# First pair's loads over two hardware queues, with a decay matrix as its mask: one change to a fused attention and feed-forward kernel

## The chip, the cores and the metric

One core of one Trainium2 chip. The metric is device time in microseconds (us), from the median of several executions. All numbers are of runs in the fast state unless a text says otherwise. "The span" is the time from the first to the last instruction in the profiled execution; it lies some 1.8 us under the time.

## The reference

Retention attention (a recurrence with one decay per head), then a feed-forward block with the activation h cos(h):

```python
B, H, S, D = 4, 8, 768, 64
gamma = 1.0 - 2.0 ** (-5.0 - arange(H));  scale = 1 / sqrt(D)
for t in range(S):
    state = gamma * state + outer(k[:, :, t], v[:, :, t])
    y[:, :, t] = scale * (q[:, :, t] @ state)
x = y.transpose(0, 2, 1, 3).reshape(3072, 512)
h = x @ w_in                      # 512 x 2048
out = (h * cos(h)) @ w_out        # 2048 x 512
```

The inputs q, k, v and the weights are fp32 in device memory; the kernel computes in bf16.

## The kernel before

The recurrence is done in chunks of 128 tokens. A *pair* is one chunk of two batches; there are 12 pairs. For each pair, q is scaled by gamma^t (`conv_q`), v by gamma^-t (`conv_v`), k only cast (`conv_k`); TensorE transposes q and k (`stage_t`), forms the scores (`stage_a`), VectorE multiplies them by a 0/1 mask (`stage_m`), TensorE makes the outputs and the running state (`stage_y`). `attend` is scores and mask products of both batches. `pair_f` and `unit_f` are the feed-forward's first product, `unit_o` its second. `warm(n)` issues n filler matmuls that are meant to keep TensorE's clock up (e6 below: 1.00 from 9 to 12 us with nine more of them, 0.50 in e5 without). Each load of q, k or v is 262 KB, in rows of 64 fp32 (256 bytes). In this text q0 is q of batch 0 of the first pair, and q0' is q of batch 0 of the second.

```python
def load(eng, p, names):                       # one DMA for each name
    ...
        eng.dma_start(out=t[SLOT[p]][b],
                      in_=src[2 * bp + b, :, ds(c * C, C)].rearrange("h t d -> t h d"))

load(nc.sync, 0, ("q0", "k0", "q1"))           # five loads on SyncE's queue
load(nc.sync, 1, ("q0", "v0"))
load(nc.gpsimd, 0, ("k1",))                    # the others on GpSimd's
...
load(nc.gpsimd, 0, ("v0", "v1"))
...
load(nc.gpsimd, 1, ("k0", "q1", "k1", "v1"))
for r in range(4):
    load_w_in(r)                               # 512 KB each after the cast
conv_v(1, nc.gpsimd)
for r in range(3):
    load_w_out(r)
...
warm(10)
conv_q(0, nc.vector)
conv_k(0, True)                                # True: on ScalarE
conv_v(0, nc.vector)
stage_t(0, False)                              # both copies on ScalarE
warm(3)
attend(0)
conv_k(1, True)
conv_q(1, nc.vector)
warm(6)
stage_y(0, nc.scalar.copy)
warm(2)
stage_t(1, None)                               # both copies on VectorE
attend(1)
pair_f(0, 0, (0,))                             # feed-forward, waits for w_in
stage_y(1, nc.scalar.copy)
pair_f(0, 0, (1,))
pair_f(1, 0)                                   # from here solid TensorE work
```

Of the kernel before, what the change touches and what calls it, by code (L numbers as in the profile page):

```python
# [10 lines left out]
FP32 = mybir.dt.float32  # L11
BF16 = mybir.dt.bfloat16
AF = mybir.ActivationFunctionType
ALU = mybir.AluOpType
# [16 lines left out]
def kernel(  # L31
# [9 lines left out]
    nc = tc.nc  # L41
    B, H, S, D = q.shape
    C = 128
    NC = S // C
# [19 lines left out]
    def sb(shape, dt, name):  # L64
        return const.tile(shape, dt, name=name)
# [6 lines left out]
    pos = sb([128, NC], FP32, "pos")  # L72
    halfpi = sb([128, 1], FP32, "halfpi")
    lnsc = sb([128, 1], FP32, "lnsc")
    sb([128, 1], FP32, "pad")

    w_in_sb = [sb([128, KIN, 512], BF16, f"w_in{r}") for r in range(4)]
    w_out_sb = sb([128, KOUT, DM], BF16, "w_out_sb")
# [19 lines left out]
    lgp = sb([128, NC, H], FP32, "lgp")  # L98
    gq = sb([128, NC, H], FP32, "gq")
    gk = sb([128, NC, H], FP32, "gk")  # L100


    SRC = {"q": (qf, q), "k": (kf, k), "v": (vf, v)}
# [3 lines left out]
    def load(eng, p, names):  # L107
        bp, c = divmod(p, NC)
        for n in names:
            t, src = SRC[n[0]]  # L110
            b = int(n[1])
            eng.dma_start(  # L112
                out=t[SLOT[p]][b],
                in_=src[2 * bp + b, :, ds(c * C, C)].rearrange("h t d -> t h d"))

    def load_w_in(r):
        nc.gpsimd.dma_start(
            out=w_in_sb[r],
            in_=moe_w_in[:, ts(r, 512)].rearrange("(i p) f -> p i f", p=128))
# [6 lines left out]
    def w_in_t(i, f):  # L126
        return w_in_sb[f // 4][:, i].rearrange("p (m j) -> p j m", j=4)[:, f % 4, :]


    load(nc.sync, 0, ("q0", "k0", "q1"))  # L130
    load(nc.sync, 1, ("q0", "v0"))
    load(nc.gpsimd, 0, ("k1",))
    nc.gpsimd.iota(pos, pattern=[[C, NC]], base=1, channel_multiplier=1,
                   allow_small_or_imprecise_dtypes=True)
    load(nc.gpsimd, 0, ("v0", "v1"))
    make_identity(nc, ident)
    nc.vector.memset(zero, 0.0)  # L137
    nc.vector.memset(lnsc, math.log(scale))
    nc.vector.memset(halfpi, math.pi / 2.0)
    nc.vector.memset(mask, 1.0)  # L140
    for h in range(H):
        nc.vector.tensor_scalar(out=lgp[:, :, h], in0=pos, scalar1=float(lg[h]),
                                scalar2=None, op0=ALU.mult)
    nc.scalar.activation(out=gq, in_=lgp, func=AF.Exp, bias=lnsc)
    nc.scalar.activation(out=gk, in_=lgp, func=AF.Exp, scale=-1.0)
    nc.scalar.activation(out=cosb[0][:, :8], in_=lgp[:, 0, :], func=AF.Sin, scale=0.0)
    for t in stb:
        nc.vector.memset(t, 0.0)
    nc.gpsimd.affine_select(out=mask, in_=mask, compare_op=ALU.is_ge, fill=0.0,
                            base=0, pattern=[[1, 128]], channel_multiplier=-1)  # L150


    def bc(g, c):
# [2 lines left out]
    def conv_q(p, eng):  # L156
        for b in range(2):
            eng.tensor_tensor(out=qs[p % NB][:, b], in0=qf[SLOT[p]][b],  # L158
                              in1=bc(gq, p % NC), op=ALU.mult)

    def conv_v(p, eng):
        for b in range(2):
            eng.tensor_tensor(out=vs[p % NB][:, b], in0=vf[SLOT[p]][b],  # L163
                              in1=bc(gk, p % NC), op=ALU.mult)
# [5 lines left out]
            else:  # L170
                nc.vector.tensor_copy(out=ks[p % NB][:, b], in_=kf[SLOT[p]][b])

    def stage_t(p, split, fill=0):
        n = p % NB
        for b in range(2):
            if fill:
                warm(fill * b)
            bank = banks.take()
            tr = bank.bitcast(BF16).rearrange("p (w a t) -> p w a t", w=2, a=HP)
            for w, src in enumerate((qs[n], ks[n])):  # L180
                for a in range(HP):
                    nc.tensor.transpose(tr[:, w, a, :], src[:, b, 2 * a : 2 * a + 2, :], ident)  # L182
            if split is None or split and b == 1:
                nc.vector.tensor_copy(out=qkt[n][:, :, b], in_=tr)  # L184
            else:
                nc.scalar.copy(out=qkt[n][:, :, b], in_=tr)
            banks.give(bank)

    def stage_t_dma(p):
        n = p % NB  # L190
# [11 lines left out]
    def stage_a(p, b):  # L202
# [8 lines left out]
                                 tile_position=(po, 0))  # L211
        return b, bk, ap

    def stage_m(p, item):
        b, bk, ap = item
        for j in range(2):
            nc.vector.tensor_tensor(  # L217
                out=am[p % 2][b][j], in0=ap[j],
                in1=mask.unsqueeze(1).to_broadcast([128, HP, 128]), op=ALU.mult)
            banks.give(bk[j])  # L220

    def stage_y(p, copy_st=nc.vector.tensor_copy):
        c = p % NC
        n = p % NB
        for b in range(2):
            bank = banks.take()
            yp = bank.rearrange("p (a t) -> p a t", a=HP)
            for a in range(HP):
                if c > 0:
                    for j in range(2):  # L230
                        nc.tensor.matmul(  # L231
                            yp[ts(j, 64), a, :], lhsT=stb[p % 2][:, b, a, ts(j, 64)],
                            rhs=qt(n, b, a), start=True, stop=False,
                            skip_group_check=True)
                for j in range(2):
                    nc.tensor.matmul(  # L236
                        yp[ts(j, 64), a, :], lhsT=vs[n][:, b, 2 * a + j, :],
                        rhs=am[p % 2][b][j][:, a, :], start=(c == 0), stop=True,
                        skip_group_check=True)
            nc.scalar.copy(out=xt[(p // 2) % 2][:, :, ts(2 * (p % 2) + b, C)], in_=yp)  # L240
            banks.give(bank)
        if c == NC - 1:
            return
        for b in range(2):
            for a in range(HP):
                for j in range(2):
                    h = 2 * a + j
                    nc.tensor.matmul(  # L248
                        st_ps[ts(j, 64), b, a, :], lhsT=ks[n][:, b, h, :],
                        rhs=vs[n][:, b, h, :], start=(c == 0 and b == 0 and a == 0),  # L250
                        stop=True, skip_group_check=True)
        for j in range(2):
            copy_st(out=stb[(p + 1) % 2][ts(j, 64), :, :, ts(j, 64)], in_=st_ps[ts(j, 64)])  # L253
# [62 lines left out]
    def warm(n):  # L316
        for _ in range(n):
            nc.tensor.matmul(spare, lhsT=zero[:, :128], rhs=zero, start=True, stop=True,  # L318
                             skip_group_check=True)
# [2 lines left out]
        for it in [stage_a(p, b) for b in range(2)]:  # L322
            stage_m(p, it)

    load(nc.gpsimd, 1, ("k0", "q1", "k1", "v1"))
    for r in range(4):
        load_w_in(r)
    conv_v(1, nc.gpsimd)
    for r in range(3):
        load_w_out(r)  # L330
    load(nc.gpsimd, 2, ("k0", "q0", "k1", "q1"))
# [2 lines left out]
    load(nc.gpsimd, 3, ("k0", "q0", "k1", "q1", "v0", "v1"))  # L334

    warm(10)
    conv_q(0, nc.vector)
    conv_k(0, True)
    conv_v(0, nc.vector)
    stage_t(0, False)  # L340
    warm(3)
    attend(0)
    conv_k(1, True)
    conv_q(1, nc.vector)
    warm(6)
    stage_y(0, nc.scalar.copy)
    warm(2)
    stage_t(1, None)
    attend(1)
    banks.give(spare)  # L350
    pair_f(0, 0, (0,))
# [8 lines left out]
    for part in range(3):  # L360
        for j in range(4):
            unit_o(0, j, part)
            if part == 2 and j == 0:
                stage_t(2, None)
                conv_v(2, nc.vector)
            elif part == 2 and j == 1:
                stage_m(2, stage_a(2, 0))
            elif part == 2 and j == 3:
                stage_m(2, stage_a(2, 1))
# [9 lines left out]
        if j == 1:  # L379
            stage_y(2, nc.scalar.copy)  # L380
    pair_f(2, 0)
    stage_t(3, None)
    pair_f(2, 1)
    attend(3)
    conv_q(4, nc.gpsimd)
# [97 lines left out]
```

## Time and profile before

| | before |
|---|---|
| time, median of 3 | 212.1 us (211.08 to 212.9) |
| span of the profiled execution | 210.7 us |
| TensorE busy | 200.9 us (95%) |
| mean granted TensorE clock | 0.99 |
| solid TensorE work begins | 20.02 us |
| TensorE's longest wait in the first 26 us | 1.5 us |

TensorE is busy 95% of the span, and without a gap worth naming from 20 us on. So the table's fifth row is the one to watch: what the first 20 us give or take should move the whole end by nearly as much. The views that show it stand in the prediction below.

### The profile page before, as it was taken

To read this page: it belongs to the slowest core of one execution; us is meant where nothing else is said; L and a number is where in the kernel's file an instruction comes from. 1 tells how busy PE (TensorE), PEld (TensorE's weight loads), DVE (VectorE), ACT (ScalarE), POOL (GpSimd) and SP (SyncE) were. 2 spreads that over 40 slices of the span, in tenths; PEclk is the share of its full clock that TensorE was granted. 3 is DMA by queue.
4 is the path that set the end of the run, shared out by engine and by line. 5 is a ranking of instruction groups with operands and counts; after the bars stand their busy time and mean duration, and the time that the engine had idled before them with its cause. 6 is when DMAs were issued, how large, how long until landed. Compare 5 with 4: busy or idle time off the path is not lost.

```text
span 210.7 us, 4125 instructions
## 1 busy us (share of the span) xinstructions
PE 200.9 (95%) x1614; PEld 113.0 (54%) x1637; DVE 115.0 (55%) x187; ACT 113.6 (54%) x183; POOL 84.3 (40%) x98
## 2 busy tenths in 40 slices
PE   7698999999999999999999999999999999999992
PEld 2357654548998554555455455445455444444440
DVE  5397686171976755859585484484482333343000
ACT  5664885219799336656745745745545554553110
POOL 7996238499968907999251500000000000000000
PEclk9889999999999999999999999999999999999999
DMA  6999999999999999999978321331101101110121
GB/s 163 325 246 206 215 260 287 341 255 334 272 190 212 213 305 243 238 284 181 321 165 200 92 63 50 87 67 50 50 3 50 50 3 50 50 50 27 74 92 60
DMA packets 55845, 33.83 MB, mean 161 GB/s; under 512 B 47249, under 2 KB 49553, under 8 KB 55825
## 3 DMA queue, kind: packets, MB, share of 16 engines
q1 hardware_dynamic: 49472, 17.70, 36.0%
q0 software_dynamic: 6208, 15.73, 29.1%
q8 instruction: 13, 0.21, 0.4%
q10 hardware_dynamic: 144, 0.13, 0.2%
q14 instruction: 8, 0.06, 0.1%
HBM read 27.26 MB, written 6.29 MB: 159 GB/s over the span
## 4 chain that ended last, share of the span: by engine, by line
PE 90%; DVE 4%; DMA 3%; issue 1%; SPq 0%; ACT 0%; DVEq 0%
PE bank L296 40%; PE bank L270 31%; PE bank L282 8%; PE bank L209 3%; DMA qf<-in_q_dram 3%; PE bank L231 2%; PE bank L236 2%; DVE am L217 2%; PE bank L182 1%; DVE qs L158 1%; PE st_ps L248 1%; PE bank L318 1%; SPq L112 0%; DVE qkt L184 0%; DVE ob L303 0%
## 5 line engine op out<-in xcount | busy, mean ns | idle before, releaser
L265 DVE TENSOR_TENSOR gt<-bank,cosb 128x512 bf16<-128x512 f32 x96 | 65.6, 690 | 63.5 <-ACT cosb L261 63.1
L261 ACT ACTIVATE cosb<-bank,halfpi 128x512 bf16<-128x512 f32 x96 | 65.4, 687 | 53.2 <-PE bank L270 41.4
L296 PE MATMUL bank<-w_out_sb,gt 128*128 128x512 bf16 x372 | 91.8, 379 | 1.1 <-issue 0.5
L270 PE MATMUL bank<-xt,w_in 128*128 128x512 bf16 x294 | 73.7, 380 | 0.4
L296 PEld LDWEIGHTS <-gt 128*128 128x128 bf16 x384 | 36.7, 98 | 42.7
L270 PEld LDWEIGHTS <-w_in 128*128 128x128 bf16 x304 | 33.8, 114 | 30.8 <-issue 0.2
L217 DVE TENSOR_TENSOR am<-bank,mask 128x512 bf16<-128x512 f32 x48 | 30.3, 682 | 1.0 <-PE bank L209 0.8
L158 POOL TENSOR_TENSOR qs<-qf,gq 128x512 bf16<-128x512 f32 x18 | 18.5, 1046 | 22.2 <-DMA qf<-in_q_dram 14.9
L308 ACT COPY ob<-bank 128x512 f32<-128x512 f32 x23 | 13.4, 586 | 23.3 <-PE bank L296 23.2
L112 POOL DMA_DIRECT2D kf<-in_k_dram x23 | 20.8, 906 | 3.2 <-DMA w_out_sb<-in_moe_w_out_dram 2.1
L163 POOL TENSOR_TENSOR vs<-vf,gk 128x512 bf16<-128x512 f32 x20 | 21.0, 1067 | 0.9 <-DMA vf<-in_v_dram 0.8
L282 PE MATMUL bank<-xt,w_in 128*128 128x256 bf16 x160 | 18.6, 273 | 0.0
L169 ACT CAST ks<-kf 128x512 bf16<-128x512 f32 x24 | 13.8, 615 | 7.3 <-DMA kf<-in_k_dram 7.3
L282 PEld LDWEIGHTS <-w_in 128*128 128x128 bf16 x160 | 17.1, 114 | 0.5
L112 POOL DMA_DIRECT2D vf<-in_v_dram x16 | 14.2, 887 | 4.3 <-DMA w_out_sb<-in_moe_w_out_dram 4.3
L240 ACT CAST xt<-bank 128x512 bf16<-128x512 f32 x24 | 13.0, 587 | 3.6 <-DVE gt L265 3.0
L236 PE MATMUL bank<-am,vs 128*64 128x128 bf16 x192 | 11.8, 220 | 0.3 <-DVE am L217 0.3
L231 PEld LDWEIGHTS <-stb 128*64 128x64 bf16 x160 | 8.7, 109 | 4.3 <-issue 3.8
L231 PE MATMUL bank<-qkt,stb 128*64 128x128 bf16 x160 | 10.6, 222 | 0.0
L236 PEld LDWEIGHTS <-vs 128*64 128x64 bf16 x192 | 10.0, 110 | 0.9 <-DVE am L217 0.4
L253 DVE CAST stb<-st_ps 64x512 bf16<-64x512 f32 x12 | 8.2, 687 | 3.5 <-PE st_ps L248 3.3
L318 PE MATMUL bank<-gt 128*128 128x512 bf16 x20 | 8.3, 565 | 1.3 <-DVE gt L137 1.3
(38 smaller groups left out, 70.6 us busy)
## 6 DMA issues: line engine op xcount, KB each, us to landing
kf<-in_k_dram POOLq DMA_DIRECT2D x23, 256.0 KB, 5.5
out_dram<-ob SPq DMA_DIRECT2D x23, 256.0 KB, 2.2
qf<-in_q_dram SPq DMA_DIRECT2D x19, 256.0 KB, 6.3
vf<-in_v_dram POOLq DMA_DIRECT2D x16, 256.0 KB, 6.2
vf<-in_v_dram SPq DMA_DIRECT2D x8, 256.0 KB, 5.7
w_in<-in_moe_w_in_dram POOLq DMA_DIRECT2D x4, 512.0 KB, 9.8
w_out_sb<-in_moe_w_out_dram POOLq DMA_DIRECT2D x4, 512.0 KB, 13.2
qf<-in_q_dram POOLq DMA_DIRECT2D x5, 256.0 KB, 6.8
```

The source lines that it names most:

```text
L112: eng.dma_start(out=t[SLOT[p]][b], in_=src[2 * bp + b, :, ds(c * C, C)].rearrange("h t d -> t h d"))
L158: eng.tensor_tensor(out=qs[p % NB][:, b], in0=qf[SLOT[p]][b], in1=bc(gq, p % NC), op=ALU.mult)
L163: eng.tensor_tensor(out=vs[p % NB][:, b], in0=vf[SLOT[p]][b], in1=bc(gk, p % NC), op=ALU.mult)
L169: nc.scalar.copy(out=ks[p % NB][:, b], in_=kf[SLOT[p]][b])
L217: nc.vector.tensor_tensor(out=am[p % 2][b][j], in0=ap[j], in1=mask.unsqueeze(1).to_broadcast([128, HP, 128]), op=ALU.mult)
L231: nc.tensor.matmul(yp[ts(j, 64), a, :], lhsT=stb[p % 2][:, b, a, ts(j, 64)], rhs=qt(n, b, a), start=True, stop=False, skip_group_check=True)
L236: nc.tensor.matmul(yp[ts(j, 64), a, :], lhsT=vs[n][:, b, 2 * a + j, :], rhs=am[p % 2][b][j][:, a, :], start=(c == 0), stop=True, skip_grou ...
L261: nc.scalar.activation(out=cb, in_=bank, func=AF.Sin, bias=halfpi)
L265: nc.vector.tensor_tensor(out=out, in0=bank, in1=cb, op=ALU.mult)
L270: nc.tensor.matmul(bank, lhsT=w_in_t(i, f), rhs=xt[g % 2][:, i, :], start=(i == 0), stop=(i == KIN - 1))
L282: nc.tensor.matmul(bank[:, ts(e, 256)], lhsT=w_in_t(i, f + e), rhs=xt[g % 2][:, i, ts(hf, 256)], start=(i == 0 and e == 0), stop=(i == KIN ...
L296: nc.tensor.matmul(bank, lhsT=gt[g % 2][:, f, ts(j, 128)], rhs=w_out_sb[:, f, :], start=(f == 0), stop=(f == KOUT - 1))
```

## The change

The intent is to start the solid stretch earlier. The first pair's q and k are loaded over two hardware queues, SyncE's and ScalarE's, two each. They are cast plainly; the scaling by gamma is put into a decay matrix by which the scores are multiplied in place of the 0/1 mask, so that no cast waits for the decay vectors. VectorE copies transposed banks as 32-bit words. GpSimd makes the decayed v of the first pair (needed for the state only; the outputs use the plain cast `vu`). The diff, cut to its core:

```diff
-    load(nc.sync, 0, ("q0", "k0", "q1"))
-    load(nc.sync, 1, ("q0", "v0"))
-    load(nc.gpsimd, 0, ("k1",))
+    load(nc.sync, 0, ("q0", "k0"))
+    load(nc.scalar, 0, ("q1", "k1"))
+    load(nc.sync, 1, ("k0", "q0"))
+    load(nc.gpsimd, 0, ("v0",))
 ...
-    load(nc.gpsimd, 0, ("v0", "v1"))
+    load(nc.gpsimd, 0, ("v1",))
+    load(nc.gpsimd, 1, ("k1", "q1", "v0", "v1"))
 ...
+    for h in range(H):
+        nc.scalar.activation(out=decay[:, h], in_=rel[:, 1], func=AF.Exp, bias=lnsc,
+                             scale=float(lg[h]))
 ...
+    def copy_bits(out, bank):
+        nc.vector.tensor_scalar(out=out.bitcast(mybir.dt.uint32),
+                                in0=bank.bitcast(mybir.dt.uint32),
+                                scalar1=0, scalar2=None, op0=ALU.bitwise_or)
 ...
     def stage_m(p, item):
-                in1=mask.unsqueeze(1).to_broadcast([128, HP, 128]), op=ALU.mult)
+            by = decay_j[:, j] if p == 0 else mask.unsqueeze(1).to_broadcast([128, HP, 128])
 ...
-    load(nc.gpsimd, 1, ("k0", "q1", "k1", "v1"))
-    for r in range(4):
-        load_w_in(r)
+    load_w_in(0)
+    conv_v(0, nc.gpsimd)
+    load_w_in(1)
     conv_v(1, nc.gpsimd)
+    load_w_in(2)
+    load_w_in(3)
 ...
-    conv_q(0, nc.vector)
-    conv_k(0, True)
-    conv_v(0, nc.vector)
-    stage_t(0, False)
-    warm(3)
+    for b in range(2):
+        nc.vector.tensor_copy(out=qs[0][:, b], in_=qf[0][b])
+    for b in range(2):
+        nc.vector.tensor_copy(out=ks[0][:, b], in_=kf[0][b])
+    for b in range(2):
+        stage_t(0, b, False)
+    for b in range(2):
+        nc.scalar.copy(out=vu[:, b], in_=vf[0][b])
+    warm(2)
     attend(0)
     conv_k(1, True)
     conv_q(1, nc.vector)
-    warm(6)
+    warm(4)
     stage_y(0, nc.scalar.copy)
+    stage_t(1, 0, False)
+    stage_t(1, 1, True)
     warm(2)
-    stage_t(1, None)
     attend(1)
```

For pairs 2 and 3 the diff only puts the 32-bit copies in place of VectorE's bf16 copies.

More of the change, by code (lines that the diff above doesn't have):

```diff
@@ L74 @@
     lnsc = sb([128, 1], FP32, "lnsc")
-    sb([128, 1], FP32, "pad")
+    lgv = sb([128, H], FP32, "lgv")
     w_in_sb = [sb([128, KIN, 512], BF16, f"w_in{r}") for r in range(4)]
@@ L100 @@
     gk = sb([128, NC, H], FP32, "gk")
+    rel = sb([128, 2, 128], FP32, "rel")
+    decay = sb([128, H, 128], FP32, "decay")
+    vu = sb([128, 2, H, D], BF16, "vu")
     SRC = {"q": (qf, q), "k": (kf, k), "v": (vf, v)}
@@ L127, in w_in_t @@
         return w_in_sb[f // 4][:, i].rearrange("p (m j) -> p j m", j=4)[:, f % 4, :]
-    load(nc.sync, 0, ("q0", "k0", "q1"))
-    load(nc.sync, 1, ("q0", "v0"))
-    load(nc.gpsimd, 0, ("k1",))
+    load(nc.sync, 0, ("q0", "k0"))
+    load(nc.scalar, 0, ("q1", "k1"))
+    load(nc.sync, 1, ("k0", "q0"))
+    load(nc.gpsimd, 0, ("v0",))
+    nc.gpsimd.iota(rel[:, 0], pattern=[[1, 128]], base=0, channel_multiplier=-1,
+                   allow_small_or_imprecise_dtypes=True)
     nc.gpsimd.iota(pos, pattern=[[C, NC]], base=1, channel_multiplier=1,
                    allow_small_or_imprecise_dtypes=True)
-    load(nc.gpsimd, 0, ("v0", "v1"))
-    make_identity(nc, ident)
+    load(nc.gpsimd, 0, ("v1",))
+    load(nc.gpsimd, 1, ("k1", "q1", "v0", "v1"))
     nc.vector.memset(zero, 0.0)
@@ L139 @@
     nc.vector.memset(halfpi, math.pi / 2.0)
-    nc.vector.memset(mask, 1.0)
     for h in range(H):
-        nc.vector.tensor_scalar(out=lgp[:, :, h], in0=pos, scalar1=float(lg[h]),
-                                scalar2=None, op0=ALU.mult)
+        nc.vector.memset(lgv[:, h : h + 1], lg[h])
+    nc.vector.tensor_scalar(out=ident, in0=rel[:, 0], scalar1=0.0, scalar2=None,
+                            op0=ALU.is_equal)
+    nc.vector.tensor_scalar(out=rel[:, 1], in0=rel[:, 0], scalar1=0.0, scalar2=1.0e6,
+                            op0=ALU.is_lt, op1=ALU.mult)
+    nc.vector.tensor_tensor(out=rel[:, 1], in0=rel[:, 1], in1=rel[:, 0], op=ALU.add)
+    nc.vector.tensor_scalar(out=mask, in0=rel[:, 0], scalar1=0.0, scalar2=None,
+                            op0=ALU.is_ge)
+    for h in range(H):
+        nc.scalar.activation(out=decay[:, h], in_=rel[:, 1], func=AF.Exp, bias=lnsc,
+                             scale=float(lg[h]))
+    nc.vector.tensor_tensor(out=lgp, in0=pos.unsqueeze(2).to_broadcast([128, NC, H]),
+                            in1=lgv.unsqueeze(1).to_broadcast([128, NC, H]), op=ALU.mult)
     nc.scalar.activation(out=gq, in_=lgp, func=AF.Exp, bias=lnsc)
@@ L148 @@
         nc.vector.memset(t, 0.0)
-    nc.gpsimd.affine_select(out=mask, in_=mask, compare_op=ALU.is_ge, fill=0.0,
-                            base=0, pattern=[[1, 128]], channel_multiplier=-1)
     def bc(g, c):
@@ L171, in conv_k, with stage_t @@
                 nc.vector.tensor_copy(out=ks[p % NB][:, b], in_=kf[SLOT[p]][b])
-    def stage_t(p, split, fill=0):
-        n = p % NB
-        for b in range(2):
-            if fill:
-                warm(fill * b)
-            bank = banks.take()
-            tr = bank.bitcast(BF16).rearrange("p (w a t) -> p w a t", w=2, a=HP)
-            for w, src in enumerate((qs[n], ks[n])):
-                for a in range(HP):
-                    nc.tensor.transpose(tr[:, w, a, :], src[:, b, 2 * a : 2 * a + 2, :], ident)
-            if split is None or split and b == 1:
-                nc.vector.tensor_copy(out=qkt[n][:, :, b], in_=tr)
-            else:
-                nc.scalar.copy(out=qkt[n][:, :, b], in_=tr)
-            banks.give(bank)
+    def copy_bits(out, bank):
+        nc.vector.tensor_scalar(out=out.bitcast(mybir.dt.uint32),
+                                in0=bank.bitcast(mybir.dt.uint32),
+                                scalar1=0, scalar2=None, op0=ALU.bitwise_or)
+    def stage_t(p, b, on_act):
+        n = p % NB
+        bank = banks.take()
+        tr = bank.bitcast(BF16).rearrange("p (w a t) -> p w a t", w=2, a=HP)
+        for w, src in enumerate((qs[n], ks[n])):
+            for a in range(HP):
+                nc.tensor.transpose(tr[:, w, a, :], src[:, b, 2 * a : 2 * a + 2, :], ident)
+        if on_act:
+            nc.scalar.copy(out=qkt[n][:, :, b], in_=tr)
+        else:
+            copy_bits(qkt[n][:, :, b], tr)
+        banks.give(bank)
     def stage_t_dma(p):
@@ L212, in stage_a @@
         return b, bk, ap
+    decay_j = decay.rearrange("p (a j) t -> p j a t", j=2)
     def stage_m(p, item):
@@ L216, in stage_m @@
         for j in range(2):
-            nc.vector.tensor_tensor(
-                out=am[p % 2][b][j], in0=ap[j],
-                in1=mask.unsqueeze(1).to_broadcast([128, HP, 128]), op=ALU.mult)
+            by = decay_j[:, j] if p == 0 else mask.unsqueeze(1).to_broadcast([128, HP, 128])
+            nc.vector.tensor_tensor(out=am[p % 2][b][j], in0=ap[j], in1=by, op=ALU.mult)
             banks.give(bk[j])
@@ L236, in stage_y @@
                     nc.tensor.matmul(
-                        yp[ts(j, 64), a, :], lhsT=vs[n][:, b, 2 * a + j, :],
+                        yp[ts(j, 64), a, :], lhsT=(vu if p == 0 else vs[n])[:, b, 2 * a + j, :],
                         rhs=am[p % 2][b][j][:, a, :], start=(c == 0), stop=True,
@@ L363 @@
             if part == 2 and j == 0:
-                stage_t(2, None)
+                stage_t(2, 0, False)
+                stage_t(2, 1, False)
                 conv_v(2, nc.vector)
@@ L381 @@
     pair_f(2, 0)
-    stage_t(3, None)
+    stage_t(3, 0, False)
+    stage_t(3, 1, False)
     pair_f(2, 1)
```

## The prediction

Two inputs of the prediction are estimates of mine that no trace had shown: 0.42 us for a plain cast by VectorE (0.36 to 0.74 us in the kernel after, 0.36 to 0.43 in e8), and a third of the rate for GpSimd's queue (from 3.2 to 6.9 us of the kernel after it moved 0.26 of 1.14 MB).

> **What bounds the kernel now.** I read first the chain of work that ended last, by share (part 4 of the page), then the same chain in order of time, then the busy time by windows, then the timeline of the first 24 us.
>
> The chain by share, before:
>
> ```profile
> PE 90%; DVE 4%; DMA 3%; issue 1%; SPq 0%; ACT 0%; DVEq 0%
> ```
>
> TensorE carries nine tenths of the end. The chain in order of time shows where the rest lies (start us, length us, what):
>
> ```profile
> 1.94 5.52 DMA qf<-in_q_dram
> ...
> 7.49 0.70 DVE qs L158
> ...
> 8.24 0.67 PE bank L182 x8
> 8.91 1.28 PE bank L318 x3
> 10.19 0.58 PE bank L209 x8
> ...
> 10.83 2.48 DVE am L217 x4
> 13.31 2.06 DVE qs L158 x2
> ...
> 15.42 0.63 PE bank L182 x8
> ...
> 16.08 0.69 DVE qkt L184
> 16.77 0.62 DVE am L217 x2
> ...
> 17.88 1.29 DVE am L217 x2
> ...
> 20.02 2.74 PE bank L282 x24
> ```
>
> Up to 20 us it is one thread: the third q/k load on SyncE's queue (q of batch 1), VectorE's scaling of it, transposes, three filler matmuls, scores, four mask products, then VectorE again for the second pair. From 20.02 us every piece is a TensorE matmul. The waits of TensorE from 20 us on are three of 0.5 us in total, and the windows (busy of PE, PEld, DVE, ACT, POOL; granted clock; DMA share; GB/s) say the same:
>
> ```profile
> 0.00:20.00 20.00, 15.46 (x173) 8.60 (x175) 13.47 (x31) 11.09 (x18) 17.40 (x27) 0.91 1.03 237
> 20.00:211.00 191.00, 185.40 (x1443) 104.39 (x1464) 101.58 (x156) 102.47 (x166) 66.91 (x71) 1.00 0.62 152
> ```
>
> So the last 190.7 us of the 210.7 us span are solid TensorE work that the change doesn't shorten. All that it can win is the moment at which the solid stretch begins. Even ten per cent of the first 20 us is 2 us, or 0.9% of the whole.
>
> [...]qs 128x512 takes 684 ns undisturbed, a 128x1024 bf16 copy out of PSUM also 684 ns.[...]the scaling of the second q of pair 1 took 1532 ns beside a GpSimd product that took 1472, against 628 and 1043 alone.[...] In the trace DMA share is at 1.03 over the first 20 us, so no bandwidth is spare.[...] The trace's granted clock was 1.00 up to 8 us, 0.50 from 9 to 12 us, 1.00 from 13 us on.
>
> **Part by part.** *Loads.* Before, SyncE issued q0, k0, q1 of the first pair; they landed at 3.9, 5.6 and 7.46 us (issue plus the time to landing), 1.75 us a piece; GpSimd brought k1 by about 6. Now SyncE has q0, k0 and ScalarE q1, k1, and GpSimd brings v. The rate from 3 us on was about 300 GB/s (windows of 1 us: 279 to 366). Four loads of 262 KB are 1.05 MB. Estimate: with two hardware queues from about 1.9 us some 0.33 MB by 3.2 us, then two thirds of 310 GB/s, since v takes the third share: 0.72 MB / 0.207 = 3.5 us. So q0 and q1 land at about 4.5 us and k0 and k1 at about 6.9, against 7.46 for the last before. The gain is 0.6 us, not more, because v's bytes now ride in front.
>
> *Casts and first copies.* Removed from the path: qs 0.70 us after 7.46, and the wait for the decay vector. Added on VectorE: four plain copies at 0.42 us. VectorE is ready for the first at about 4.9 us: GpSimd's 128x128 iota ends at about 2.8, then four 128x128 ops at 0.2 us, the product for the decay exponents 0.2 and two memsets at 0.49 each. Three copies hide behind loads; the last ends at 6.9 + 0.42 = 7.35. Transposes of batch 1 end at 7.75. Before, ScalarE copied each transposed bank in 1.01 us, the last from 8.94 to 9.95. Now VectorE does both as 512 words, for which I take the 0.68 us of a 128x512 fp32 read of PSUM (mask products). They follow each other: 7.4 to 8.1, 8.1 to 8.75. Two fillers (one fewer) at 0.43 fit beside them. Scores run from about 8.6, so the mask products start at 8.95 instead of 10.83: **1.9 us won** at this point. The 32-bit form is not faster than VectorE's own bf16 copy (684 ns each); against ScalarE it is 0.33 us.
>
> *Decay matrix.* Eight Exp over 128x128 on ScalarE. From gq (48 elements, 335 ns) and gk following it (226 ns) I estimate 0.29 us each, 2.4 us. They start behind two DMA issues (about 0.5 us each, as on SyncE) and the 1.28 us table load, at 3.4 us, and end at 5.9, then gq, gk, the Sin table and by 8 us the plain casts of v, two of 0.62. All is done by 9.2 us, before the mask products or their matmuls ask. The products read an fp32 mask now[...]: 4 x 0.62 = 2.5 us, as before. They end at 11.4 instead of 13.31.
>
> *Second pair.* VectorE's two scalings, 11.4 to 12.7 if alone. GpSimd now makes vs of pair 0 after the first weight issue (about 8.3 to 10.5) and of pair 1 when its v lands (about 12 to 14), so one of VectorE's two will again be stretched to about 1.5 us; before, that cost 2.06 for the two. I take the same 2.06: 13.45. The first bank's copy follows on VectorE (0.68) while ScalarE copies the second (1.01). ScalarE has xt and stb to copy first, about 2.2 us from 11.9, so the second is ready at about 14.9 to 15.2. Before, the second copy ended at 16.77. Mask products: 14.3 to 15.6 and 15.6 to 16.9, at worst 17.2, against 19.17. Against the 1.9 us won I give back 0.2 for ScalarE's second copy: **1.7 us**.
>
> *Elsewhere.* Three fewer fillers of 0.2 to 0.43 us on TensorE; they stood in waits, so nothing comes of it directly. Pairs 2 and 3: VectorE's two copies each change from 684 ns to about the same, beside solid TensorE work: nothing.
>
> Sum: 212.1 - 1.7 = **210.4 us**, 0.8% faster.
>
> **The rivals.** *A, the weights become the wait.* The first w_in block is needed when pair 0's feed-forward starts, at 17.15 us before. Its landing is issue 8.80 plus the shortest of the four times to landing, 6.9, so about 15.7. As much data stands in front of it as before. If attention of pair 1 were free by then, the 1.06 us of feed-forward matmuls would end at 16.76, and the second pair's outputs could run on without their stall of 0.53: 18.15 + 0.53 - 16.76 = 1.9 us is the most that can be won, unless the block lands sooner.[...] For it: GpSimd is nearly fully busy up to 20 us. Against: the products stand behind the issue of the first block, and the second block (landed 18.56, needed 22.8) has over 4 us of slack. Time: 210.2 to 211.2.
>
> *B, the loads share worse.* Three queues from the start, with no more bandwidth: if GpSimd's queue takes half, k1 lands at about 8.5 and the casts wait. Then the copies end at 10.4, past the 9.95 of before, and what is left is little: 211.5 to 212.3.
>
> *C, the clock.* With three fewer fillers TensorE may stay at half clock past 12 us. Transposes, scores and outputs of pair 1 together are about 3 us at full clock, half hidden behind VectorE; it costs 0.5 to 1.5 us: 211 to 212. Against: TensorE is nearly gapless from 7.4 to 11 us in my schedule.
>
> *D, all better:* k lands at 6.2 and no contention: 2.4 us, 209.7.
>
> **Range and chances.** The central sum has the greater weight, about half; A a quarter; B and C a fifth together. Two per cent is 4.2 us, which would ask the solid stretch to begin at 15.8, as the first weights land: nearly impossible. A loss of 4.2 us would need a new wait of 6 us. The three runs before spread over 1.8 us, so the range is wide on both sides: 208.9 to 212.1. Faster by over 2%: 0.03; within: 0.95; slower: 0.02.
>
> **What would show it.** Right: k1 of pair 0 landed near 7 us; VectorE's plain copies near 0.42 us; copies of transposes near 0.68; the first am product near 9 us; the run of 24 matmuls of the feed-forward that begins at 20.02 now near 18.3; TensorE's busy time after it unchanged. Rival A shows as TensorE waiting for w_in before the first feed-forward matmul, B as VectorE waiting for kf past 8 us, C as a clock of 0.50 past 13 us. The prediction is wrong if the solid stretch begins after 20 us or before 17, or if TensorE gets new waits later.

## The result, and the profile after

| | before | after |
|---|---|---|
| time, median of 4 | 212.5 us (211.08 to 213.47) | 218.75 us (218.23 to 219.25) |
| span of the profiled execution | 210.7 us | 216.4 us |
| mean granted clock | 0.99 | 0.976 |
| first mask product begins | 10.83 us | 10.08 us |
| first transpose of the second pair begins | 14.38 us | 18.90 us |
| solid TensorE work begins | 20.02 us | 25.56 us |

The ratio is 1.030, with a 95% interval from 1.023 to 1.037: slower by 3%. A ratio here, and in every experiment, is the one on record, taken over the fast runs of both kernels, so it is not quite the ratio of the medians quoted. A ratio whose interval reaches across 1.02 (e2 and e4) is clearly above 1, but whether it is over 2% stays unclear.

The chain that ended last, by share of the span, of the kernel after:

```profile
PE 86%; DMA 7%; DVE 3%; SPq 1%; ACT 0%; issue 0%; DVEq 0%; ACTq 0%
```

A DMA now holds 7% of the chain where one held 3% before; 7% of 216.4 us is 15 us. The same chain in order of time (start us, length us, what) says which:

```profile
2.70 15.36 DMA qf<-in_q_dram
...
18.16 0.70 DVE qs L172
18.86 0.05 issue
18.90 1.89 PE bank L198 x16
20.79 0.85 PE bank L335 x2
...
25.56 2.74 PE bank L299 x24
```

This is q0', SyncE's fourth load and the sixth load on the hardware queues. It is issued at 2.70 us, lands at 18.06, and all of VectorE's and TensorE's work on the second pair stands behind it. TensorE's longest waits in the first 26 us (engine, line, what it waited for: us in total, times, longest us), before:

```profile
PE bank L182 <- DVE qs L158: 1.9, 2, 1.5
PE bank L318 <- DVE gt L137: 1.3, 1, 1.3
```

and after:

```profile
PE bank L198 <- DVE qs L172: 5.5, 1, 5.5
PE bank L198 <- DVE ks L359: 1.5, 1, 1.5
```

The wait is put down to VectorE's scaling, but that is 0.70 us long; the chain shows that it started when the load landed. One should always follow such a wait one step further back.

The windows of the kernel after (length, then busy us of PE, PEld, DVE, ACT and POOL, each with its count, then the granted clock, DMA share and GB/s) show the hole and what follows it:

```profile
13.00:18.10 5.10, 0.45 (x21) 0.34 (x16) 0.00 (x0) 1.95 (x4) 5.10 (x8) 0.83 1.23 199
18.10:24.00 5.90, 5.10 (x46) 3.66 (x48) 3.77 (x6) 1.01 (x1) 2.10 (x3) 0.56 1.23 211
25.56:216.00 190.44, 186.87 (x1464) 104.28 (x1464) 102.42 (x156) 102.43 (x166) 65.84 (x69) 1.00 0.60 147
```

From 13.0 to 18.1 us TensorE does 0.45 us of work and VectorE none. Then TensorE works, but at a clock of 0.56; that this comes from the idle time before it is shown by e11 below (fillers in that time, and 1.00 from 18.1 to 24 us). From 25.56 us it is the old solid stretch: 216.4 - 25.56 = 190.8 us here, 210.7 - 20.02 = 190.7 in the kernel before. So nearly the whole loss of 5.7 us between these two executions is in the delay of that stretch, 5.54 us, and it splits in two: the second pair's transposes begin 18.90 - 14.38 = 4.52 us later, and from there to the solid stretch it takes 6.66 us in place of 5.64, 1.02 us more.

**Why the load took 15 us.** The DMA queues by window say it (queue, kind: packets, MB, share of the 16 engines' time). q1 is SyncE's queue, q10 ScalarE's, q0 GpSimd's. From 0 to 9 us, before:

```profile
q1 hardware_dynamic: 4766, 1.20, 59.0%
q0 software_dynamic: 245, 0.81, 26.1%
```

and after:

```profile
q1 hardware_dynamic: 2988, 0.76, 37.0%
q10 hardware_dynamic: 2080, 0.52, 25.8%
q0 software_dynamic: 231, 0.80, 24.6%
```

Two hardware queues moved 0.76 + 0.52 = 1.28 MB where one had moved 1.20. The second queue shared the rate out anew and added hardly any. From 9 to 12 us, before:

```profile
q0 software_dynamic: 282, 0.95, 92.7%
q1 hardware_dynamic: 434, 0.11, 16.0%
```

and after:

```profile
q0 software_dynamic: 309, 0.84, 89.2%
q1 hardware_dynamic: 428, 0.11, 17.5%
```

These look alike, but before, SyncE's queue ran out: of its 434 packets 415 went by 10 us. After, it had a whole load left. From 12 to 13 us in the kernel after:

```profile
q0 software_dynamic: 153, 0.16, 91.8%
q1 hardware_dynamic: 153, 0.04, 29.6%
```

Both queues got 153 packets. A packet of SyncE's queue is one row of 256 bytes (0.04 MB over 153), one of GpSimd's about 1 KB here. The counts agree within two from 11 to 15 us (121 for SyncE's and 119 for GpSimd's, then 153 and 153, 155 and 153, 159 and 157); from 9 to 11 us SyncE's queue got more than one for one (135 to 98, 172 to 92), and at the end of the load fewer (146 to 167, then 103 to 171). That the queues take turns, a packet each, is inferred from these counts and not shown by itself. Either way SyncE's queue got only 0.02 to 0.04 MB/us from 8 to 17 us, while GpSimd's queue was never empty (its packets took 88 to 103% of the DMA engines' time in each of these microseconds), as the weights follow the loads without a gap. That the short rows are what makes its share of the bytes so small is argued from these counts; no run changed the size of a row.

The account closes. Six hardware loads are 1.57 MB. 1.28 MB had moved by 9 us and 0.11 MB more by 12, so some 0.18 MB was due at 12 us. From 12.0 to 18.5 us the same view has 744 packets, 0.19 MB, for q1. Before, five hardware loads were 1.31 MB: 1.20 by 9 us and 0.11 from 9 to 12. The fifth just got through.

### The profile page after: what moved, and what is told of

Read it like the earlier page. It is cut to its first block, busy times and chain, and to the rows that moved or that the text cites. A ratio compares the mean times of both kernels' runs of the same rounds, so it can differ in the third digit from the quotient of the medians.

```text
span 216.4 us, 4156 instructions
## 1 busy us (share of the span) xinstructions
PE 203.7 (94%) x1634; PEld 114.1 (53%) x1634; DVE 115.7 (53%) x192; ACT 114.8 (53%) x190; POOL 84.9 (39%) x97
## 4 chain that ended last, share of the span: by engine, by line
PE 86%; DMA 7%; DVE 3%; SPq 1%; ACT 0%; issue 0%; DVEq 0%; ACTq 0%
PE bank L313 38%; PE bank L287 31%; DMA qf<-in_q_dram 7%; PE bank L299 7%; PE bank L225 3%; PE bank L248 2%; PE bank L253 2%; DVE qkt L188 1%; PE bank L198 1%; DVE am L236 1%; PE st_ps L265 1%; SPq L115 1%; PE bank L335 0%; DVE qs L172 0%; ACT cosb L278 0%
## 5 line engine op out<-in xcount | busy, mean ns | idle before, releaser
L313 PE MATMUL bank<-w_out_sb,gt 128*128 128x512 bf16 x384 | 93.3, 379 | 0.0
L287 PE MATMUL bank<-xt,w_in 128*128 128x512 bf16 x304 | 75.1, 380 | 0.0
L236 DVE TENSOR_TENSOR am<-bank,mask 128x512 bf16<-128x512 f32 x44 | 27.8, 682 | 1.8 <-PE bank L225 1.8
L177 POOL TENSOR_TENSOR vs<-vf,gk 128x512 bf16<-128x512 f32 x22 | 22.6, 1047 | 1.3 <-DMA vf<-in_v_dram 1.3
L115 POOL DMA_DIRECT2D kf<-in_k_dram x21 | 18.9, 902 | 2.1 <-DMA w_out_sb<-in_moe_w_out_dram 1.6
L115 POOL DMA_DIRECT2D vf<-in_v_dram x17 | 15.2, 895 | 9.0 <-DVE vs L177 4.3
L299 PEld LDWEIGHTS <-w_in 128*128 128x128 bf16 x160 | 17.3, 114 | 0.8 <-issue 0.2
L183 ACT CAST ks<-kf 128x512 bf16<-128x512 f32 x22 | 12.4, 615 | 2.2 <-DMA kf<-in_k_dram 2.1
L253 PE MATMUL bank<-am,vs 128*64 128x128 bf16 x176 | 10.9, 219 | 0.1
L253 PEld LDWEIGHTS <-vs 128*64 128x64 bf16 x176 | 9.4, 110 | 0.4 <-issue 0.4
```

Source lines behind the costliest of these rows:

```text
L115: eng.dma_start(out=t[SLOT[p]][b], in_=src[2 * bp + b, :, ds(c * C, C)].rearrange("h t d -> t h d"))
L177: eng.tensor_tensor(out=vs[p % NB][:, b], in0=vf[SLOT[p]][b], in1=bc(gk, p % NC), op=ALU.mult)
L236: nc.vector.tensor_tensor(out=am[p % 2][b][j], in0=ap[j], in1=by, op=ALU.mult)
L253: nc.tensor.matmul(yp[ts(j, 64), a, :], lhsT=(vu if p == 0 else vs[n])[:, b, 2 * a + j, :], rhs=am[p % 2][b][j][:, a, :], start=(c == 0), ...
L287: nc.tensor.matmul(bank, lhsT=w_in_t(i, f), rhs=xt[g % 2][:, i, :], start=(i == 0), stop=(i == KIN - 1))
L299: nc.tensor.matmul(bank[:, ts(e, 256)], lhsT=w_in_t(i, f + e), rhs=xt[g % 2][:, i, ts(hf, 256)], start=(i == 0 and e == 0), stop=(i == KIN ...
```

## The experiments

The theory: the sixth hardware load doesn't fit in front of the moment at which GpSimd's queue is full, and then gets a packet for a packet (153 for 153 from 12 to 13 us above). The rivals: that the other parts of the change (casts, decay matrix, GpSimd's products) cost the time; that the order or the queue of the loads matters and not their number; that the clock is the cause and not a consequence.

### e1: q0' back on GpSimd's queue

```diff
-    load(nc.sync, 1, ("k0", "q0"))
+    load(nc.sync, 1, ("k0",))
...
-    load(nc.gpsimd, 1, ("k1", "q1", "v0", "v1"))
+    load(nc.gpsimd, 1, ("q0", "k1", "q1", "v0", "v1"))
```

> The changed kernel, but q of batch 0 of the second pair is loaded by GpSimd (first of its second-pair loads) instead of being SyncE's fourth load. Theory S (the sixth load of the hardware queues falls behind GpSimd's queue, which from 8 us on is never empty; packets go one for one, 256 bytes against 1 to 3 KB): the load lands by 11 us, VectorE's second-pair scaling starts near 12.5 instead of 18.2, the clock doesn't halve a second time, and the time falls by 6 to 8 us to 210 to 212, at or a little under the kernel before. Rival G (GpSimd is overloaded by the decayed v and its queue is late anyway): the stall moves to this or another second-pair load, time stays above 215. Rival C (fewer fillers let the clock fall, and the rest follows): second half-clock stretch stays, time above 215.

Measured: 212.77 us beside 212.39 for the kernel before, ratio 1.003 (1.001 to 1.005). q0' landed at 9.8 us and the 5.5 us wait was gone. One load moved from one queue to another takes back all but 0.3% of the 3%. It isn't clean, and the time lies above the 210 to 212 expected: the last of the five hardware loads, k0', landed at 13.5 us, ScalarE waited 4.05 us for it, and the solid stretch began at 20.41. Its chain has that load:

```profile
1.92 11.55 DMA kf<-in_k_dram
```

SyncE's queue had 243 packets left at 8 us; 185 of them went by 10 us, and the last 21 took from 11 to 13.5. So one packet for one is not the whole story: the tail of a load is slower still, and why is not shown.

### e2: the new loads alone, in the kernel before

The kernel before, with the load lines of the change and nothing else of it (`conv_v(1)` and the weights stay where they were).

> The kernel before with nothing but the new distribution of the first loads (six on the hardware queues of SyncE and ScalarE). Theory S: the sixth, q of batch 0 of the second pair, lands at 16 to 19 us, TensorE waits for it, time 216 to 220. Rival G and rival C: none of their parts is in, so it stays at 211 to 213.5.

Measured: 216.1 us, ratio 1.021 (1.014 to 1.028). Two lines of its chain (start us, length us, what):

```profile
3.28 13.99 DMA qf<-in_q_dram
17.29 0.70 DVE qs L159
```

The distribution of loads by itself makes the same load late (it landed at 17.3 us, in the change at 18.06), and costs 2.1% without any cast, decay matrix or GpSimd product of the change.

### e3: the change with the old loads

The kernel after, with the load lines of before (pair 1's loads on GpSimd stay as early as in the change).

> The changed kernel with the old distribution of the first loads (five on SyncE's queue, seven on GpSimd's), all else as changed. Theory S: no second-pair load lands after 13.5 us, no TensorE gap over 2 us after 13 us; time 210.5 to 212.5. Rival G or C: time stays above 215.

Measured: 212.4 us, ratio 0.9996 (0.997 to 1.002). The other side of e2: all of the change but its loads costs nothing, and gains nothing that can be measured. The solid stretch of its profile began at 19.32 us, 0.7 earlier than before, with a span of 210.6. One of its four runs was slow and is not in the ratio.

### e4: the sixth load on ScalarE's queue

```diff
-    load(nc.sync, 1, ("k0", "q0"))
+    load(nc.sync, 1, ("k0",))
+    load(nc.scalar, 1, ("q0",))
```

> The changed kernel with the sixth hardware load moved from fourth on SyncE's queue to third on ScalarE's, so that the two late loads stand in two hardware queues. If every queue gets a packet per round (theory S), they move side by side at about 0.04 MB per us each, and the load lands near 13 us instead of 18; time 211 to 214. If the hardware queues share one rate between them (about 0.04 MB per us in all), it lands near 18 and the time stays at 217 to 219.

Measured: 216.83 us, ratio 1.022 (1.019 to 1.025); q0' landed at 16.5 us. Both sizes that I had written down missed. From 12 to 13 us its queues were:

```profile
q0 software_dynamic: 153, 0.16, 91.3%
q10 hardware_dynamic: 156, 0.04, 30.1%
```

So the equal counts are ScalarE's as well, and carrying the load on the other hardware queue doesn't cure it. It landed 1.6 us sooner than in the change. Some 1 us of this was won before 8 us, by when 5130 hardware packets had moved, against 4977 in the change (an estimate, from the 153 packets a microsecond that follow); from 8 to 12 us the two hardware queues together moved 413 + 96 = 509 packets, no more than SyncE's alone in the change (519). SyncE's tail was too short, 96 packets, to tell whether two late hardware loads get a turn each or share one rate, so that question of mine stays open. My 13 us had taken the load as half done by 8 us, when it had hardly begun.

### e5: only the first pair on the hardware queues

```diff
-    load(nc.sync, 1, ("k0", "q0"))
...
-    load(nc.gpsimd, 1, ("k1", "q1", "v0", "v1"))
+    load(nc.gpsimd, 1, ("k0", "q0", "k1", "q1", "v0", "v1"))
```

> The changed kernel with only q and k of the first pair on the hardware queues (two each) and everything of the second pair by GpSimd. The previous step (five on the hardware queues) left k of batch 0 of the second pair landing at 13.5 us, and 212.8 us. If lateness comes only from hardware-queue packets that are left when GpSimd's queue is full, all second-pair loads land by 13.5 and in the order of issue (k0 by 10.5, q0 by 11), first-pair loads unchanged (k1 at 7.6), and the time is 210.5 to 212. If GpSimd's queue is no better, a second-pair load still lands after 13.5 in front of a wait, and the time stays near 212.8.

Measured: 214.38 us, ratio 1.007 (1.005 to 1.010), above the 210.5 to 212 expected. The loads did come in order: k0' at 9.0, q0' at 9.8, k1' at 10.5, q1' at 11.3. But the solid stretch began at 21.63. Now it was VectorE (start us, busy us, engine, line, what):

```profile
12.56 2.05 POOL L176 TENSOR_TENSOR vs<-vf,gk 128x512 bf16<-128x512 f32 x2
12.72 3.06 DVE L171 TENSOR_TENSOR qs<-qf,gq 128x512 bf16<-128x512 f32 x2
```

VectorE's two scalings of q' took 3.06 us beside GpSimd's two of v'; in the kernel after, where GpSimd made no product at that time, they took 1.29. This looks like the collision that the prediction had named for the second pair, larger than its 2.06; e9, e10 and e12 below test it, and find that the product is not all of it.

### e8: GpSimd's later loads held back

The kernel after with its six hardware loads as they are; GpSimd makes the first pair's decayed v before it issues any load of the second pair or a weight.

```diff
-    load(nc.gpsimd, 1, ("k1", "q1", "v0", "v1"))
...
-    load_w_in(0)
     conv_v(0, nc.gpsimd)
+    load(nc.gpsimd, 1, ("k1", "q1", "v0", "v1"))
+    load_w_in(0)
```

> The changed kernel with its six hardware loads as they are, but GpSimd makes the decayed v of the first pair before it issues its four second-pair loads (so its queue is empty from about 8 to 11 us), and the weights after them. Theory S: the same sixth load, same queue and place, lands by 11 us instead of 18, since nothing shares with it; the second-pair loads by GpSimd land at 14 to 17 and the first weights at 18 to 19, so the whole is still 213 to 217. Against theory S: it lands at 16 us or later in spite of an empty GpSimd queue.

Its queues from 8 to 9 us:

```profile
q1 hardware_dynamic: 889, 0.22, 99.3%
q0 software_dynamic: 27, 0.05, 14.4%
```

The kernel after in the same microsecond:

```profile
q0 software_dynamic: 98, 0.32, 95.6%
q1 hardware_dynamic: 91, 0.02, 10.6%
```

Both kernels had moved about as many hardware packets by 8 us (4896 here, 4977 in the kernel after). With GpSimd's queue nearly empty SyncE's moves 0.22 MB in that microsecond, with it full 0.02. The same sixth load landed 6.9 us after its issue, at 10.0 us instead of 18.06. This is the sharpest test of the cause: nothing about the load itself was changed, only what stands in the other queue. The time, 218.6 us, ratio 1.030 (1.026 to 1.034), missed the 213 to 217 that I expected, because the price was paid elsewhere: the first w_in block landed at 21.45 us, and TensorE waited 3.1 us for it. Bytes kept out of one wait were taken from another.

### e11: fillers in the stall

The kernel after, with `warm(24)` ahead of the second pair's transposes, to separate the wait from the clock that drops in it.

> The changed kernel with 24 filler matmuls in the stall of TensorE before the second pair's transposes, nothing else. The stall itself ends with the load at 18.1 us as before. If the second half-clock stretch (17 to 23 us in the changed kernel) comes from that idle stall, it goes, and the transposes and scores after it run in half the time: 0.8 to 1.5 us less, 217.2 to 218. If it doesn't, the time stays at 218.75.

Its windows (columns as above):

```profile
13.00:18.10 5.10, 4.52 (x47) 2.34 (x47) 2.02 (x4) 2.58 (x5) 5.10 (x8) 0.96 1.22 198
18.10:24.00 5.90, 5.22 (x51) 2.99 (x50) 3.31 (x6) 1.01 (x1) 1.99 (x3) 1.00 1.23 212
```

Measured: 217.9 us, ratio 1.026 (1.021 to 1.030). The clock was 0.50 from 10 to 13 us and 1.00 from 14 us on, through the wait and after it, and from the second pair's first transpose to the solid stretch it took 5.03 us in place of 6.66. So the dropped clock explains the 1.02 us above and a little more, and not the wait: VectorE still got q0' only at 18.6 us. The fillers ran from 15.87 to 20.99 us, past the landing, which ate most of the gain. They came that late because in this profile the two casts of k of the first pair took 3.10 us (7.28 to 10.38), where they took 1.34 in the kernel after, though up to there the two kernels are the same. GpSimd was busy for 0.98 and 1.00 us of the two microseconds from 8 us on; what held the casts up is not shown. The intervals of this kernel and the kernel after overlap, so the time alone decides nothing.

### e6, e7, e9, e10, e12: to win what the change was for

All start from e5. e6 puts 9 fillers into the first pair's transposes:

```diff
+            if w == 0:
+                warm(fill)
...
-        stage_t(0, b, False)
+        stage_t(0, b, False, (7, 2)[b])
```

> As the previous run, plus nine filler matmuls inside the first transposes (seven before k of batch 0, two before k of batch 1), which stand in the wait for k's load. If the half clock from 8 to 14 us in the runs with five loads comes from TensorE's idle 2 us before k lands, the clock stays at 1.00 from 5 to 14 us, the first scores and transposes take half as long, and the time falls by 0.5 to 1 us against the run without fillers. If the clock is set by something else, it halves as before and the fillers change nothing or cost up to 0.5 us.

Measured: 214.31 us, ratio 1.009 (1.005 to 1.012). The clock was 1.00 from 8 to 16 us, against 0.50 from 9 to 12 us in e5, so the fillers did what they were for, and the time didn't move; the 0.5 to 1 us expected did not come.

e7 is e6 with the first pair's casts of k on ScalarE:

```diff
+    for b in range(2):
+        nc.scalar.copy(out=ks[0][:, b], in_=kf[0][b])
...
-    for b in range(2):
-        nc.vector.tensor_copy(out=ks[0][:, b], in_=kf[0][b])
```

> As the previous run, but the two plain casts of k of the first pair on ScalarE, behind the eight decay exponentials, instead of on VectorE. On VectorE they took 0.58 and 0.63 us in the changed kernel and up to 1.49 us in the run with q0 by GpSimd, against 0.36 us for an undisturbed one of q. If that is GpSimd[...], the casts on ScalarE take a steady 0.62 us each, the second ends at about 8.2, and the time is 0 to 0.7 us below the run before it. If the casts were slow for another cause, no gain, or a loss from the later v casts (they now end near 11).

Measured: 214.36 us, ratio 1.009 (1.006 to 1.012). The pair of q' scalings took 3.25 us and still sat on the path.

e10 (built on e5) and e9 (built on e7) move GpSimd's `conv_v(1)` behind the last w_in issue:

```diff
     load_w_in(1)
-    conv_v(1, nc.gpsimd)
     load_w_in(2)
     load_w_in(3)
+    conv_v(1, nc.gpsimd)
```

> The run with four hardware loads and no other edit, with the same move of the second pair's v. The block of 3.06 us for two products at 12.7 us goes to 1.3, the second pair's transposes start near 13.4 instead of 15.2, time 212 to 213 instead of 214.4. The difference to the run above is what fillers and the casts on ScalarE are worth once nothing behind them blocks: 0.3 to 1 us; if none, the half clock of the first scores costs nothing.

> The run with four hardware loads, nine fillers and k's casts on ScalarE, and now GpSimd's decayed v of the second pair moved behind the issue of the last two w_in blocks. In that earlier run VectorE's scaling of the second pair's q took 3.25 us for two products at 12.5 us while GpSimd made v (12.56 to 14.6). If the two block each other[...], the pair now takes 1.3 us, the second pair's transposes start near 13.3 instead of 15.2, and the time falls by 1.5 to 2.5 us to 211.8 to 212.8, or, if the clock then also stays up, to 210.5. If the products were slow for another reason, nothing changes (214.3).

Measured: e10 214.17 us, ratio 1.008 (1.005 to 1.011); e9 214.21 us, ratio 1.008 (1.005 to 1.011). GpSimd's product began at 14.0 us in e9, late but not late enough: the q' pair still took 3.47 us. In e10 the two took 1.25 and 1.98 us. So moving the product by two issues wins nothing, against the 1.4 to 2.5 us expected. e12 is e9 with the product behind two w_out issues as well:

> As the run with four hardware loads, fillers, k's casts on ScalarE and v after w_in, but GpSimd's v of the second pair now stands behind two w_out issues too, from about 15.3 us, when VectorE's two q products should be over. In the run before, v began at 14.0 and the second q product (13.7) still took 1.98 us beside it, so that run didn't test the block. If the block is the cause of what is left, the two q products take 1.3 to 1.9 us, the second pair's transposes are over by 14.5 instead of 16.7, the solid stretch begins near 18.7 (20.0 in the kernel before), and the time is 210.5 to 212 against 212.4 for the kernel before and 214.2 for the run before. If not, it stays above 213.5.

Measured: 213.13 us, ratio 1.001 (0.999 to 1.003), against e9's 1.008, but above the 210.5 to 212 expected; the solid stretch began at 20.42. A line of its chain:

```profile
12.92 2.71 DVE qs L173 x2
```

The two scalings take 2.71 us on the path still. The first, 1.33 us, ended at 14.2, before GpSimd's product began at 15.07; beside it stood only issues of weight loads. So GpSimd's product is not the only thing that stretches them. Why weight issues should disturb VectorE's product here and not its product of v in the kernel before (0.69 us at 9.32 us, beside weight issues that lasted from 8.80 to 11.8) or in e13 below (0.68 us each, beside weight issues from 13.71 to 16.02), I have not settled.

### e13, e14: the products swapped

If VectorE's q' product is disturbed by GpSimd (3.25 us for the two in e7, 1.29 in the kernel after), the product on the path can be given to GpSimd and the one off it to VectorE. e13, on e7:

```diff
     conv_v(0, nc.gpsimd)
+    conv_q(1, nc.gpsimd)
     load_w_in(1)
-    conv_v(1, nc.gpsimd)
...
-    conv_q(1, nc.vector)
...
     stage_t(1, 0, False)
+    conv_v(1, nc.vector)
     stage_t(1, 1, True)
```

> As the run with four hardware loads, fillers and k's casts on ScalarE (214.4 us), but for the second pair GpSimd scales q (behind the first pair's v, about 11.8 to 13.9 us, while VectorE only reads banks) and VectorE makes the decayed v after it has copied the first transposed bank. If VectorE's held-up q product was what ate the gain, the second pair's transposes are over by 14.4 us instead of 16.7, the solid stretch begins at 18.3 to 19, and the time is 210.3 to 211.8, below the kernel before. If not, the solid stretch still begins after 20 us and the time stays above 212.5.

e14 is the same with `conv_q(1, nc.gpsimd)` behind `load_w_in(1)`:

> As the other run of this pair, but the second w_in block is issued ahead of GpSimd's q product (which then runs 0.8 us later). If late weights are what bounds after the exchange, this one is the faster by 0.3 us or more; if q's product bounds, it is 0.3 to 0.8 us slower.

Measured: e13 212.12 us beside 212.41, ratio 1.000 (0.997 to 1.003); e14 212.17 us, ratio 0.999 (0.997 to 1.001). e13 was expected below 211.8, and of the two outcomes that I had written down for e14 neither came: the two agree, so neither the weights nor q's product is shown to bound. Two lines of e13's chain:

```profile
14.61 1.28 DVE vs L178 x2
...
19.14 2.74 PE bank L302 x24
```

VectorE's two products of v' take 1.28 us, undisturbed, and the solid stretch begins at 19.14 us, 0.88 before that of the kernel before. The span of this profile is 210.2 us against 210.7, so some 0.4 of the 0.88 were lost again later. Nor does e13 beat the best executions of the kernel before, whose spans in the same rounds lie between 209.4 and 212.0, while all but two of e13's 14 lie between 210.1 and 210.5. No version was found that beats the kernel before; e13 and e14 equal it. (The profiled execution of e14 was in the slow state and is not read here.)

## Why the prediction was wrong

The prediction was 210.4 us with a range up to 212.1, and "within 2%" at 0.95. It came out at 218.75 us, 3% slower.

**What bounds the kernel: right.** The last 190 us are unchanged to 0.1 us, and nearly the whole difference lies in where they begin. The sentence that named 20 us as the limit of being wrong was the one that caught it: they began at 25.56.

**Loads of the first pair: nearly right.** q0 and q1 landed at 4.45 and 4.94 us (predicted 4.5), k0 and k1 at 6.86 and 7.56 (predicted 6.9). The estimate of 0.33 MB by 3.2 us was high, 0.21 MB had moved. (Two slips in the working: the rate from 3 us on lay between 272 and 366 GB/s, not 279 and 366, and 3.2 + 3.5 us gives 6.7, not 6.9.)

**The step that failed: "Loads" stopped at the first pair.** It followed four loads, 1.05 MB, and never the fifth and sixth, k0' and q0', which stand behind them on SyncE's queue. "Second pair" then let VectorE's scalings of q' start at 11.4 us as if q0' had landed. It landed at 18.06, and TensorE waited 5.5 us. ("A loss of 4.2 us would need a new wait of 6 us", the prediction says; this was nearly that wait.) To see it blind, one had to add up the hardware bytes (1.57 MB against 1.31 before), see that 1.2 MB had moved by 9 us in the kernel before, and ask what the rest gets when GpSimd's queue is full. The kernel before could raise the question but not answer it: its five loads were just through when GpSimd's queue filled at about 10 us. I had written that no bandwidth was spare, and used it only for the four loads.

**Casts, copies and first mask product: the mechanism right, the size off.** The plain cast was put at 0.42 us, with no trace behind the figure. It took 0.36 for the first of q, 0.74 for the second, and 0.58 and 0.63 for k's two. GpSimd was issuing loads beside all four, the fast one too. e8 points to these issues: there GpSimd issued nothing from 3.6 us to its product at 7.7, and the four casts took 0.36 to 0.43 us. The 32-bit copy was 0.67 us (0.68 predicted), decay's eight Exp 2.45 us (2.4), the four mask products with the fp32 decay matrix 2.48 us, as with the bf16 mask before (2.48). The first mask product began at 10.08 us, 0.75 before that of the kernel before, and not 1.9: k1 was 0.66 us later than predicted, its cast 0.21 us longer, and the first scores took 0.60 us in place of 0.35, as TensorE's clock fell to 0.50 at about 9.65 us. Up to here a gain was left; the wait for q0' undid it.

**The gain of 1.7 us: not there even without the stall.** e3, with the old loads, starts its solid stretch 0.7 us earlier and its time is the same; e13 starts 0.88 earlier and gains nothing in the mean. In these profiles the solid stretch, which the prediction held fixed, was a little longer: 191.3 us in e3 (210.6 - 19.32) and 191.1 in e13, against 190.7 before. Why is open. With the stall cured at its source by e5, the two scalings that I had priced at 2.06 us took 3.06.

**The rivals.** A, the weights, did not happen: w_in's first block landed at 15.5 us as predicted (15.7), and only e8, which held it back, made TensorE wait for it. B, the queue shares, was the right family, for the wrong load: it named k1, whose delay came to 0.66 us. C, the clock, was right in its sign (0.50 past 13 us: from about 16.5 to 23.3) and is a consequence: e11 holds the clock at 1.00 from 14 us on and keeps the wait. It costs about 1 us of the 5.54.

**What is shown and what is argued.** That the load distribution causes the loss is shown from both sides (e2 alone costs 2.1%, e3 without it nothing), that the sixth load is what waits by e1, and that GpSimd's full queue makes it slow by e8. e2's 2.1% is less than the change's 3.0%; the rest agrees with its load landing 0.8 us sooner and its solid stretch beginning at 23.93 us in place of 25.56, but no run separates that further. That the small packets are what makes the share so small, and why the tail of a load is slower than one packet for one (e1), is not shown.

## What to carry to other kernels

Before moving loads between queues, add up the bytes of each queue up to the moment at which the other one is full, and follow every load that moved, not only those that the change is about: here the last one in line paid (15.36 us on the chain). In these runs a load of 256-byte rows on a hardware queue was not slowed by half when a steady stream of larger packets began on GpSimd's queue, but from 0.22 MB/us (e8, 8 to 9 us) to 0.02 to 0.04 (the kernel after, 8 to 17 us). Look at the packets of each queue as well as at its bytes: from 12 to 13 us of the kernel after the counts were equal, 153 and 153, and the bytes 0.04 and 0.16 MB. When TensorE waits for a short op, look at what that op had waited for.

## What these runs measured of the hardware

- Two DMA queues side by side: in the kernel after, 153 packets of SyncE's queue for 153 of GpSimd's from 12 to 13 us, but 172 for 92 from 10 to 11. What the profile counts as a packet was here a single row of 256 bytes on SyncE's and ScalarE's queues (744 for 0.19 MB), and 1 to 3 KB on GpSimd's (153 for 0.16 MB, 309 for 0.84 MB). A hardware queue with such rows got 0.02 to 0.04 MB/us beside a full GpSimd queue (8 to 17 us of the kernel after), 0.22 beside a nearly empty one (8 to 9 us of e8).
- VectorE beside GpSimd: VectorE's plain cast of 128x512 took 0.36 us at its shortest, 0.58 to 0.74 otherwise in the kernel after, up to 1.49 us in e1; e11's two casts of k took 3.10 us together. A product of VectorE with both inputs in SBUF took 0.69 us undisturbed, 1.53 us beside a GpSimd product in the kernel before, and in e12 the first of two took 1.33 us beside GpSimd's issues of weight loads with no GpSimd product running. This is not settled (0.69 us beside such issues in the kernel before).
- Copies of a transposed bank by VectorE: 512 32-bit words took 0.67 us in the kernel after, the same bank as 1024 bf16 elements 0.684 us in the kernel before. ScalarE's copy took 1.01 us.
- TensorE's clock: it was 0.50 from about 8.7 to 12.1 us in the kernel before, though TensorE's longest wait until then was 1.5 us (6.8 to 8.2), with short work on both sides. In the kernel after it fell at about 9.65 us, and again at about 16.5 us, 3 us into the stall that began at 13.46. With nine fillers in the waits of the first pair (e6) it was 1.00 from 9 to 12 us, where e5 had 0.50. How idle TensorE must be, and for how long, before its clock falls is not shown.
